# Chunks of 64 tokens in four 64x64 quadrants, two batches per step, in a written program order

## The chip, the cores and the metric

The kernel runs on one core of one Trainium2 chip. The metric is the device time of one execution in microseconds (us). Before the change, three runs took 906.59, 907.54 and 913.81 us (median 907.54). The profile comes from one further execution.

## What is computed

Two stages follow each other. The first is a recurrence over 768 tokens for 4 batches and 8 heads with a 40x40 state each; the second is a feed-forward block on the 3072 rows of 320 values that the first leaves. All inputs are fp32, except the two weight matrices, which arrive as 64-bit floats.

```python
for t in range(S):
    y[:, :, t] = einsum('bhd,bhde->bhe', r_t, state)
    Sa = einsum('bhde,bhe->bhd', state, a_t)
    state = state * w_t[:, :, None, :] - einsum('bhd,bhe->bhde', Sa, b_t)
    state = state + einsum('bhd,bhe->bhde', v_t, k_t)
x = y.transpose(0, 2, 1, 3).reshape(B * S, H * D)
h = x @ w_in                      # 320 -> 1024
solu = h * softmax(h)
ln = (solu - mean) / sqrt(var + 1e-6) * g_ln
out = ln @ w_out                  # 1024 -> 320
```

## The kernel before

The recurrence is done in chunks. Inside a chunk of 128 tokens of one batch, cumulated decays turn it into products of matrices, one triangular system per head, and a state that goes from chunk to chunk. There are 4 batches of 6 chunks, so 24 steps; consecutive steps belong to different batches.

`load` and `decay` (L240, L260) bring a chunk's inputs and make cumulated decays: `pcum` and `pcx` on TensorE, exp on ACT, and the scaled keys `kb` on GpSimd (L280). `front` (L289) transposes a and b, multiplies them to the triangular matrices `nt` with `scores`, and sends `ax`, `kb` and `nt` to DRAM. The four 32x32 diagonal blocks of each of the 8 heads go into `blk_dram`; four chunks fill its 128 rows. `invert` (L322) reads such a batch back and inverts all its blocks at once on VectorE, 30 columns with two instructions each (L336, L338), and stores the inverse `u` and its transpose. `bring` (L350) fetches everything for a chunk again. `solve` (L385) completes the 128x128 inverses from the 32x32 ones by products in 32x32 and 64x64 tiles (`py`, `pz`; L398, L424, L431). `attend` makes kT, vT, rT and the masked products `psi` and `lamv`. `recurrence` (L437) carries the state: `px`, `pu`, `pnu`, `plamu`, `pst`. `readout` (L487) makes the chunk's output `pyo`, scales it, and moves it into `xT` by DMA.

The feed-forward block is `hidden` (L510: `h` in 12 matmul records, a maximum, exp, product, statistics, normalised rows) and `output` (L544: eight transposes `plnT`, then `po` in 16 records).

`weights` (L186) fetches the two matrices in pieces on ACT's DMA queue and `narrow` (L141) turns their 64-bit words into fp32 with instructions on VectorE, GpSimd and ACT in turn. Two buffers hold the landing words.

The main loop starts several of these as generators and takes one part of each in turn. A scheduler then orders the instructions of each engine when the program is built; the only constraints written out are a barrier after the first four fronts and `tc.issue_after(inverted[0])`, which holds the weights' conversion until the first inversion is through. All of the chunk's DMAs are issued by SyncE (SP). PSUM has six single banks in rotation and one pair for `h`.

Of the kernel before, what the change touches and what calls it, by code (L numbers as in the profile page):

```python
# [16 lines left out]
P = 128  # L17
Q = 32
TILE_HEADS = ((0, 1, 6), (2, 3, 7), (4, 5))
GRP = 4  # L20
AHEAD = 6
LAG = 3
# [3 lines left out]
def shape_constants():  # L26

    s, t = np.arange(P)[:, None], np.arange(P)[None, :]
    first = (s < P // 2).astype(np.float64)
    parts = dict(
        ident=np.eye(P),
        tri=s < t,
        cum_in=first - (s <= t),
        cum_ex=(s < t) - first,  # L40
        half=np.concatenate([1 - first, first], 1),
    )
    at, where = 0, {}
    for name, x in parts.items():
        where[name] = (at, at + x.shape[1])
        at += x.shape[1]
    return np.concatenate([np.asarray(x, np.float64) for x in parts.values()], 1).astype(np.float32), where
# [3 lines left out]
def kernel(  # L51
# [18 lines left out]


# [4 lines left out]
    G = H // 2  # L76
    NCH = S // P
    N = B * NCH
    NF = DFF // P
    NK, KT = 3, 3 * D  # L80
    assert (H, D, S % P, DFF) == (8, 40, 0, 1024)

    const = ctx.enter_context(tc.tile_pool(name="const", bufs=1))
    raw = ctx.enter_context(tc.tile_pool(name="raw", bufs=2))
    two = ctx.enter_context(tc.tile_pool(name="two", bufs=2))
    small = ctx.enter_context(tc.tile_pool(name="small", bufs=4))
    dram = ctx.enter_context(tc.tile_pool(name="dram", bufs=AHEAD + 2, space=bass.MemoryType.DRAM))
    ps1 = ctx.enter_context(tc.tile_pool(name="ps1", bufs=6, space=PSUM))
    ps2 = ctx.enter_context(tc.tile_pool(name="ps2", bufs=1, space=PSUM))

    nc.scalar.preload_act_table_set(LN_EXP)

    def zeroed(engine, name, shape, n, pad=False):

        tiles = []
        for i in range(n):
            x = const.tile(shape, FP32, name=f"{name}{i}")
            if pad:
                flat = x if len(shape) == 3 else x.rearrange("p j h c -> p (j h) c")
                engine.memset(flat[:, :, D:64], 0.0)  # L100
            else:
                engine.memset(x, 0.0)
            tiles.append(x)
        return tiles

# [12 lines left out]


    lw_t = zeroed(nc.gpsimd, "lw", [P, H, 64], 2, True)  # L120
    a_t = zeroed(nc.gpsimd, "a", [P, H, 64], 2, True)
    kb_t = zeroed(nc.gpsimd, "kb", [P, 2, H, 64], 2, True)
    rv_t = zeroed(nc.vector, "rv", [P, 2, H, 64], 3, True)
    x0_t = zeroed(nc.vector, "x0", [P, H, 64], 2, True)
    ti_t = zeroed(nc.vector, "tinvT", [P, 2, G, P], 2)
    tn_t = zeroed(nc.vector, "tinv", [P, 2, G, 64], 2)
    sm_t = zeroed(nc.vector, "sm", [P, G, 2, 64], 2)
    st_t = [const.tile([P, G, D], FP32, name=f"st{i}") for i in range(B)]
    nu_t = [const.tile([P, H, 64], FP32, name=f"nu{i}") for i in range(2)]
    y_mid = const.tile([P, 2, G, Q], FP32, name="y_mid")  # L130
    y_last = const.tile([P, 2, G, 64], FP32, name="y_last")
    AXW = 2 * P + 2
# [7 lines left out]

    def narrow(dst, bits):  # L141


# [23 lines left out]
    def load_weight(dst, parts, step):  # L167

# [11 lines left out]
        if wide_:  # L180
            for lo in range(0, width, step):
                with tc.issue_after(inverted[0]):
                    narrow(dst[:, lo:lo + step], to[:, lo:lo + step])
                yield

    def weights():  # L186
# [8 lines left out]
        for c in range(NF):  # L195
            yield from load_weight(w2[:, c, :], [moe_w_out[c * P:(c + 1) * P, :]], DM)
            nc.gpsimd.tensor_scalar(out=w2[:, c], in0=w2[:, c], scalar1=g_col[:, c:c + 1],
                                    scalar2=None, op0=ALU.mult)

    def half(p):  # L200
        return slice(64 * p, 64 * p + 64)

    def pair(t, g):
        return t[:, 2 * g:2 * g + 2, :].rearrange("p a b -> p (a b)")
# [4 lines left out]
    def transposed(name, src, tag="T", bufs=3):  # L209

        t = bank("p" + name)
        for g in range(G):
            nc.tensor.transpose(out=t[:, g * P:(g + 1) * P], in_=pair(src, g), identity=ident)  # L213
        o = two.tile([P, G, P], FP32, tag=tag, name=name, bufs=bufs)
        nc.scalar.copy(out=o.rearrange("p g t -> p (g t)"), in_=t)  # L215
        return o

    def scores(name, lhs, rhs, dst):

        t = [bank("p" + name) for p in range(2)]  # L220
        for g in range(G):
            for p in range(2):
                nc.tensor.matmul(t[p][:, g * P:(g + 1) * P], lhsT=lhs[half(p), g, :],  # L223
                                 rhs=rhs[half(p), g, 0:P], start=True, stop=True)
        for p in range(2):
            nc.vector.tensor_tensor(  # L226
                out=dst[:, p], in0=t[p].rearrange("q (g c) -> q g c", g=G),
                in1=tri.unsqueeze(1).to_broadcast([P, G, P]), op=ALU.mult)

    def wide(name, bufs=2):  # L230
        return two.tile([P, 2, G, P], FP32, tag=name, name=name, bufs=bufs)

    st = [dict() for _ in range(N)]
    blocks, inverse, inverted = {}, {}, []

    def where_(i):
        ci, bi = divmod(i, B)
        return bi, ci

    def load(i, late=False, others=nc.sync):  # L240
        if i >= N:
            return
        bi, ci = where_(i)

        def src(ap):
            return ap[bi, :, ci * P:(ci + 1) * P, :].rearrange("h t d -> t h d")

        d = st[i]
        if late:
            rv = d["rv"] = rv_t[i % 3]  # L250
            nc.sync.dma_start(out=rv[:, 1, :, 0:D], in_=src(v))
            nc.sync.dma_start(out=rv[:, 0, :, 0:D], in_=src(r))
            return
        for n, ap, queue in (("w", w, nc.sync), ("b", b, nc.sync), ("k", k, others)):
            d["raw_" + n] = raw.tile([P, H, D], FP32, tag="raw_" + n, name="raw_" + n)
            queue.dma_start(out=d["raw_" + n], in_=src(ap))
        d["a"] = a_t[i % 2]
        others.dma_start(out=d["a"][:, :, 0:D], in_=src(a))

    def decay(i):  # L260

        d = st[i]
        lw, kb = lw_t[i % 2], kb_t[i % 2]
        d["kb"] = kb
        nc.scalar.activation(out=lw[:, :, 0:D], in_=d["raw_w"], func=AF.Ln)
        ax = d["ax"] = two.tile([P, G, AXW], FP32, tag="ax", name="ax")
        inv = two.tile([P, DM], FP32, tag="inv", name="inv")
        t = bank("pcum")
        nc.tensor.matmul(t[:, 0:DM], lhsT=c_("cum_in"), rhs=lw[:, :, 0:D], start=True, stop=True)
        nc.scalar.activation(out=inv, in_=t[:, 0:DM], func=AF.Exp)  # L270
        lo = where["cum_ex"][0]
        for j in range(2):
            t = bank("pcx")
            for g in range(2):
                nc.tensor.matmul(t[:, g * 130:g * 130 + 130], lhsT=pair(lw, 2 * j + g), rhs=cst[:, lo:lo + 130],
                                 start=True, stop=True)
            nc.scalar.activation(out=ax[:, 2 * j:2 * j + 2, P:], in_=t[:, 0:260].rearrange("p (g t) -> p g t", g=2),
                                 func=AF.Exp)
        for j, n in enumerate("kb"):
            nc.gpsimd.tensor_tensor(out=kb[:, j, :, 0:D], in0=d["raw_" + n], in1=heads(inv), op=ALU.mult)  # L280
    def quarter(q):
        return slice(Q * q, Q * q + Q)

    def homes(i, q):

        at = (i % GRP) * 32 + q * H
        return slice(at, at + H)

    def front(i):  # L289

        d = st[i]
        decay(i)
        yield
        ax = d["ax"]
        t = bank("paT")
        for g in range(G):
            nc.tensor.transpose(out=t[:, g * P:(g + 1) * P], in_=pair(d["a"], g), identity=ident)
        nc.vector.tensor_tensor(out=ax[:, :, 0:P], in0=t.rearrange("p (g t) -> p g t", g=G), in1=ax[:, :, P:2 * P],
                                op=ALU.mult)
        bT = transposed("bT", d["kb"][:, 1])  # L300
        d["ax_dram"] = dram.tile([P, G, AXW], FP32, tag="ax_dram", name="ax_dram")
        nc.sync.dma_start(out=d["ax_dram"], in_=ax)
        d["kb_dram"] = dram.tile([P, 2, H, 64], FP32, tag="kb_dram", name="kb_dram")
        nc.sync.dma_start(out=d["kb_dram"], in_=d["kb"])
        yield
        nt = wide("nt")
        scores("nt", bT, d["ax"], nt)
        load(i + 2)
        yield
        n = i // GRP  # L310
        if i % GRP == 0:
            blocks[n] = dram.tile([P, Q, Q], FP32, tag="blk_dram", name="blk_dram", bufs=2)
        for q in range(4):
            nc.sync.dma_start(out=blocks[n][homes(i, q)].rearrange("h s t -> s h t"),
                              in_=nt[quarter(q), :, :, quarter(q)].rearrange("s p g t -> s (p g) t"))
# [280 lines left out]
    for i in range(N):  # L596
# [4 lines left out]
        if more:  # L601
            bring(i + 1)
# [44 lines left out]
```

## Time and profile before

| | |
|---|---|
| median of the runs | 907.54 us |
| span of the profiled execution | 908.3 us |
| TensorE (PE) busy | 784.1 us, 86% |
| VectorE (DVE) busy | 487.9 us, 54% |
| ScalarE (ACT) / GpSimd (POOL) busy | 262.9 / 135.9 us |
| DMA engines, mean busy share 387 to 515 us | 0.62 |
| first `px`, last `po` records | 123.3 us, 904.5 us |
| a step between 258.8 and 706.2 us | 31.95 us |

The profiled execution took 908.3 us from first to last instruction, which is also its time. A line of a group reads: source line, engine, operation, output<-inputs, shapes, count, then busy time in us and mean ns of one, then the engine's idle time before these and what ended it. PEld is TensorE's weight load, which overlaps PE. In the chain of what ended last, each line is start, length in us, and what ran or was waited for. The clock of TensorE is a share of full speed.

### The profile page before, as it was taken

The page shows a single profiled execution, that of the slowest core. Times are in us where ns is not written, and L with a number is a line of the kernel's source. Part 1 is how long each engine was busy: PE and PEld are TensorE (multiplying, and loading weights), DVE is VectorE, ACT ScalarE, POOL GpSimd, SP SyncE. Part 2 cuts the span into 40 slices and gives each one's busy share as a digit, 9 for nine tenths or more (in the row PEclk, how much of TensorE's full clock was granted, in tenths as well). Part 3 has the DMA queues.
Part 4 walks back from the last instruction along what each step waited for, and adds up shares of the span by engine and source line. Part 5 has one row for each costly group of instructions (what it writes and reads, how often), then busy time and mean ns, then how long its engine had stood idle before and what let it go on. Part 6 is the DMA issues. An engine that isn't in the chain of part 4 may idle for free.

```text
span 908.3 us, 20640 instructions
## 1 busy us (share of the span) xinstructions
PE 784.1 (86%) x8481; PEld 605.8 (67%) x8481; DVE 487.9 (54%) x1088; ACT 262.9 (29%) x566; POOL 135.9 (15%) x176
## 2 busy tenths in 40 slices
PE   5440387885999999999999999999999999999985
PEld 4330275664877787687778678777777887776643
DVE  4139575594432795543794345965337944325322
ACT  2110342321333233243233323233232323322211
POOL 2112567211011002001001100110110010000000
PEclk9855577997899999999999999999999999999987
DMA  9996678564575745667456576545645244210000
GB/s 193 223 196 158 157 188 200 130 156 135 115 168 114 198 98 179 141 129 163 126 143 172 123 173 139 144 144 123 147 117 146 70 105 101 67 63 15 8 15 14
DMA packets 276093, 117.95 MB, mean 130 GB/s; under 512 B 251160, under 2 KB 258080, under 8 KB 276000
## 3 DMA queue, kind: packets, MB, share of 16 engines
q1 hardware_dynamic: 269728, 110.47, 50.8%
q10 hardware_dynamic: 6272, 6.17, 2.7%
q8 instruction: 67, 1.10, 0.5%
q14 instruction: 26, 0.21, 0.1%
HBM read 68.52 MB, written 44.14 MB: 124 GB/s over the span
## 4 chain that ended last, share of the span: by engine, by line
PE 61%; DVE 15%; DMA 9%; issue 5%; POOL 4%; SPq 3%; ACT 2%; POOLq 0%; ACTq 0%; DVEq 0%
PE po L558 12%; PE h L517 10%; DVE u L338 4%; PE pyo L498 4%; DVE prod L336 4%; PE px L451 4%; PE plnT L553 3%; DMA kbx<-kb_dram 3%; PE py L424 2%; PE ppsi L223 2%; PE pyo L494 2%; PE pnt L223 2%; PE pu L458 2%; PE pst L474 2%; DMA bits<-in_moe_w_out_dram 2%
## 5 line engine op out<-in xcount | busy, mean ns | idle before, releaser
L517 PE MATMUL h<-w_in,xT 120*128 120x512 f32 (+1 forms) x288 | 148.3, 641 | 9.5 <-issue 5.7
L558 PE MATMUL po<-w,lnT 128*128 128x320 f32 x384 | 111.4, 444 | 0.0
L226 DVE TENSOR_TENSOR psi<-ppsi,cst 128x512 f32<-128x512 f32 x48 | 30.9, 684 | 122.1 <-PE ppsi L223 122.1
L558 PEld LDWEIGHTS po<-w,lnT 128*128 128x128 f32 x384 | 72.3, 193 | 30.1 <-issue 2.4
L517 PEld LDWEIGHTS h<-w_in,xT 120*128 120x128 f32 (+1 forms) x288 | 51.6, 197 | 54.5 <-issue 49.9
L539 POOL TENSOR_TENSOR rs<-c,mhalf 128x1 f32<-128x1 f32 x24 | 13.2, 549 | 428.7 <-DVE c L538 428.7
L521 DVE TENSOR_REDUCE nmax<-h 128x1 f32<-128x1024 f32 x24 | 29.4, 1223 | 72.0 <-PE h L517 72.0
L213 PE MATMUL pkT<-cst,kbx 128*128 128x128 f32 x96 | 16.3, 295 | 57.0 <-DMA kbx<-kb_dram 55.4
L338 DVE TENSOR_TENSOR u<-u,prod 128x30 f32<-128x30 f32 (+9 forms) x180 | 62.4, 347 | 4.6
L336 DVE TENSOR_TENSOR prod<-blk,u 128x30 f32<-128x30 f32 (+9 forms) x180 | 61.7, 343 | 5.1
L213 PEld LDWEIGHTS pkT<-cst,kbx 128*128 128x128 f32 x96 | 11.9, 150 | 69.4 <-issue 58.9
L215 ACT COPY kT<-pkT 128x512 f32<-128x512 f32 x24 | 14.0, 585 | 133.1 <-PE pkT L213 131.9
L554 ACT COPY lnT<-plnT 128x512 f32<-128x512 f32 x48 | 26.0, 588 | 90.3 <-PE plnT L553 90.3
L451 PE MATMUL px<-rv,psi 128*128 128x40 f32 x384 | 47.7, 286 | 0.0
L451 PEld LDWEIGHTS px<-rv,psi 128*128 128x128 f32 x384 | 46.8, 199 | 0.0
L280 POOL TENSOR_TENSOR kb<-raw_k,inv 128x320 f32<-128x320 f32 x24 | 21.0, 874 | 162.5 <-issue 113.0
L498 PE MATMUL pyo<-lamv,kbx 128*64 128x128 f32 x384 | 42.2, 282 | 0.0
L498 PE MATMUL pyo<-lamu,kbx 128*64 128x128 f32 x384 | 41.0, 273 | 0.0
L433 DVE TENSOR_SCALAR tinvT<-pz 64x256 f32<-64x256 f32 x48 | 19.7, 413 | 36.6 <-PE pz L431 36.0
L223 PE MATMUL pnt<-ax,bT 64*128 64x128 f32 x384 | 31.2, 297 | 7.5 <-ACT bT L215 3.9
L226 DVE TENSOR_TENSOR lamv<-plamv,cst 128x512 f32<-128x512 f32 x48 | 30.9, 684 | 11.1 <-PE plamv L223 11.1
L424 PEld LDWEIGHTS py<-tinv,ntx 64*64 64x64 f32 x384 | 25.6, 142 | 16.7 <-issue 9.1
(110 smaller groups left out, 1549.7 us busy)
## 6 DMA issues: line engine op xcount, KB each, us to landing
ax_dram<-ax SPq DMA_DIRECT2D x24, 516.0 KB
axx<-ax_dram SPq DMA_DIRECT2D x24, 516.0 KB
kb_dram<-kb SPq DMA_DIRECT2D x24, 512.0 KB
kbx<-kb_dram SPq DMA_DIRECT2D x24, 512.0 KB
nt_dram<-nt SPq DMA_DIRECT2D x24, 192.0 KB
ntx<-nt_dram SPq DMA_DIRECT2D x24, 192.0 KB
raw_w<-in_w_dram SPq DMA_DIRECT2D x24, 160.0 KB
raw_b<-in_b_dram SPq DMA_DIRECT2D x24, 160.0 KB
```

The source lines that it names most:

```text
L213: nc.tensor.transpose(out=t[:, g * P:(g + 1) * P], in_=pair(src, g), identity=ident)
L223: nc.tensor.matmul(t[p][:, g * P:(g + 1) * P], lhsT=lhs[half(p), g, :], rhs=rhs[half(p), g, 0:P], start=True, stop=True)
L226: nc.vector.tensor_tensor(out=dst[:, p], in0=t[p].rearrange("q (g c) -> q g c", g=G), in1=tri.unsqueeze(1).to_broadcast([P, G, P]), op=ALU ...
L336: nc.vector.tensor_tensor(out=t, in0=nb[:, j:j + 1, j + 1:Q].to_broadcast([P, j, m]), in1=u[:, 0:j, j:j + 1].to_broadcast([P, j, m]), op=A ...
L338: last = nc.vector.tensor_tensor(out=u[:, 0:j, j + 1:Q], in0=u[:, 0:j, j + 1:Q], in1=t, op=ALU.subtract)
L424: nc.tensor.matmul(t[hi, g * 64:g * 64 + 64], lhsT=nt[lo, G * p + g, 32:96], rhs=tinv[lo, p, g, :], start=True, stop=True)
L451: nc.tensor.matmul(t[:, h * D:h * D + D], lhsT=d["psi"][:, h % 2, h // 2, :], rhs=vb[:, h, 0:D], start=not ci and h == 0, stop=True, skip_ ...
L498: nc.tensor.matmul(t[half(h % 2), h // 2 * P:h // 2 * P + P], lhsT=kb[:, j, h, :], rhs=lam[:, h % 2, h // 2, :], start=not ci and h < 2 an ...
L517: nc.tensor.matmul(h[:, hh], lhsT=d["xT"][0:n, kt, :], rhs=w_in[0:n, kt, hh], start=kt == 0, stop=kt == NK - 1)
L521: nc.vector.tensor_reduce(out=nmax, in_=h, axis=AX.X, op=ALU.max, negate=True)
L553: nc.tensor.transpose(out=t[:, j * P:(j + 1) * P], in_=ln[:, f * P:(f + 1) * P], identity=ident)
L558: nc.tensor.matmul(o[:, 0:DM], lhsT=lnT[:, f, :], rhs=w2[:, f, :], start=f == 0, stop=f == NF - 1)
```

## The change

A chunk is now 64 tokens, and one step takes the same chunk of two batches, one on partitions 0 to 63 and one on 64 to 127. Again there are 24 steps: two pairs of batches in turn, 12 chunks each. Every product between 64-token matrices is 64x64 (contraction of 40 or 64) and is addressed to one of TensorE's four quadrants; `in_turn` orders 16 such products so that the four quadrants alternate. There are 13 groups of 16 in a full step (`carried`, `norm`, `driven`, `solved` twice, `couple`, `answered`, `scores` twice, `read` three times, `close`).

With 64 tokens the inverse has two 32x32 diagonal blocks and one off-diagonal block, so one `couple` and one `close` complete it. `nt`, the transposed a and the decays stay in SBUF; only `kb` makes the round trip through DRAM. The state is no longer scaled to mid-chunk: decays count from the chunk's start, and the state's transposes are made by `states`. The state update is read off the same PSUM tile as the output (`read`, columns 64 to 103).

Loads are split by batch and, for v and r, by head parity: 16 DMAs for the six inputs instead of six. `invert` keeps its arithmetic and its four-chunk batches; its pieces are called by `some` at fixed places. Normalisation after the statistics is left out of VectorE: the mean over 1024 is taken out of `w2` once, and 1/sqrt is applied by ACT as it copies `po`.

The pools run under `manual_schedule`: all engines execute in the order in which the Python code issues. `fence` puts a marker on GpSimd between groups that write one PSUM tile from different quadrants.

```diff
-AHEAD = 6
-LAG = 3
+C = 64
+AHEAD = 7
+    ctx.enter_context(tc.manual_schedule())
...
+    units = [(p, g, q, h) for g in range(2) for p in range(2) for q in range(2) for h in range(2)]
+    def in_turn(tile_of, some=units):
+        lots = {}
+        for u in some:
+            lots.setdefault(tile_of(*u), []).append(u)
+        lots = list(lots.values())
+        return [lot[n] for n in range(max(map(len, lots))) for lot in lots if n < len(lot)]
...
+    def fence(tiles):
+        for t in tiles:
+            nc.gpsimd.keepalive_nop([nc.gpsimd.lower_ap(t[:, 0:512])])
...
+    def fetch(i):
+        d["kb"] = two.tile([P, 2 * H, C], FP32, tag="kbx", name="kbx")
+        nc.sync.dma_start(out=d["kb"], in_=d["kb_dram"])
...
+    def driven(i):
+        for u in in_turn(lambda p, g, q, h: (p, p ^ h)):
+            p, g, q, h = u
+            j = 2 * g + q
+            mm(d["px"][h][half(p ^ h), j * D:j * D + D], d["psi"][half(p), h, j],
+               d["lv"][half(p), 4 * h + 2 * g + q, C:], start=(h, p ^ h) not in d["opened"])
+            d["opened"].add((h, p ^ h))
...
+    first = -(AHEAD + 2)
+    for i in range(first, N + 2):
+        j = i + AHEAD
+        n, at = divmod(j, GRP)
+        early = i < 0
+        if i == first:
+            load_keys(0)
+            load_keys(1)
+        carried(i)
+        norm(j)
+        driven(i)
+        load_keys(j + 3)
+        load_values(i + 2)
+        spread(j)
+        if ok(j) and at == GRP - 1:
+            inv[0] = invert(n)
+            some(1)
+        folded(i - 2)
+        attend(i + 1)
+        some(3)
+        fetch(i + 2)
+        output(i - 2)
+        solved(i)
+        couple(i + 1)
+        some(3)
+        hidden(i - 1)
+        answered(i)
+        weighed(i - 1)
+        scores(i + 1)
+        spreadof(i - 1)
+        some(3)
+        front(j + 1)
+        decay(j + 2)
+        states(i + 1)
+        some(3)
+        if early:
+            drawn(5)
+        read(i, True)
+        close(i + 1)
+        read(i, False)
+        leave(i)
+        if (i + 2) % GRP == 0:
+            some(40)
+        if i == -1:
+            drawn(100)
+        bring(i + 2)
```

In it, `spread` sends a chunk's diagonal blocks to `blk_dram`; the first piece of `invert` (`some(1)`) loads a full batch and makes `u<-blk` on VectorE; `folded` and `output` are the two halves of the old `output`; `weighed` and `spreadof` are the product and the statistics of the old `hidden`; `leave` scales the output, issues the four `xT` DMAs and updates the state (sums on VectorE, product on GpSimd); `drawn` takes pieces of `weights`; `bring` fetches a chunk's inverse blocks. Step i also does the front for chunk i + 8, and the feed-forward block for chunks i - 1 and i - 2.

## The prediction

> **What bounds the kernel now.** I read the page first, then the windows by stage, the chain of one steady step, the groups of instructions by line, and SyncE's timeline. The page names the busy engine:
>
> ```profile
> span 908.3 us, 20640 instructions
> ...
> PE 784.1 (86%) x8481; PEld 605.8 (67%) x8481; DVE 487.9 (54%) x1088; ACT 262.9 (29%) x566; POOL 135.9 (15%) x176
> ```
>
> By stage (columns: window, length, busy PE, PEld, DVE, ACT, POOL with counts, TensorE clock, DMA share, GB/s):
>
> ```profile
> 90.00:125.00 35.00, 17.32 (x180) 15.92 (x180) 21.84 (x58) 10.89 (x29) 19.34 (x22) 0.51 0.73 165
> 125.00:160.00 35.00, 26.78 (x323) 21.02 (x323) 23.52 (x54) 13.36 (x33) 26.15 (x25) 0.85 0.76 189
> 450.00:482.00 32.00, 31.51 (x366) 24.94 (x366) 26.59 (x68) 10.72 (x24) 5.42 (x6) 1.00 0.57 152
> ```
>
> Up to about 165 us the weights, which arrive as 64-bit words, are made into fp32; TensorE waits. From 258.8 to 706.2 (the starts of px L451 in the chain) 14 steps take 31.95 us each, and TensorE is busy all of it. So a steady step is worth what its TensorE instructions cost. The chain inside one step (start, length, what):
>
> ```profile
> 468.09 0.63 PE pz L398 x48
> 468.72 4.50 PE po L558 x16
> 473.23 1.07 PE py L424 x16
> 474.30 1.05 PE h L517 x2
> 475.35 1.07 PE pz L431 x16
> 476.43 3.63 PE h L517 x8
> 480.06 0.44 PE pkT L213 x4
> ```
>
> An fp32 product leaves two records, a transpose one. In one 64x64 quadrant a record costs 1.07/16 = 67 ns. The 32x32 products that go round three tiles cost 0.63/48 = 13 ns, so records of different tiles do overlap. The large products, 4.5 (po) and 5.5 (h), stay. Vector work and SyncE's issues:
>
> ```profile
> L226 DVE TENSOR_TENSOR psi<-ppsi,cst 128x512 f32<-128x512 f32 x48 | 30.9, 684 | 122.1 <-PE ppsi L223 122.1
> ...
> L338 DVE TENSOR_TENSOR u<-u,prod 128x30 f32<-128x30 f32 (+9 forms) x180 | 62.4, 347 | 4.6
> L336 DVE TENSOR_TENSOR prod<-blk,u 128x30 f32<-128x30 f32 (+9 forms) x180 | 61.7, 343 | 5.1
> ```
>
> ```profile
> 404.18 0.83 SPq L506 DMA_DIRECT2D xT<-x  x1
> ...
> 410.33 0.37 SPq L369 DMA_DIRECT2D kbx<-kb_dram  x1
> 410.79 1.39 SPq L356 DMA_DIRECT2D tinv<-ut_dram  x3
> ```
>
> An issue costs SyncE 0.37 to 0.83 us. In the chain, blocks land 2.0 us after the issue (tinv, 736.6) and 512 KB 4.0 us (kbx, 218.3).
>
> **What the skill says.** The Trainium skill, "TensorEngine Tiling (Array Packing)", Key Properties: tiles load weights and multiply in parallel, and a change of tiling mode drains the array. The 13 ns agree with the first; no row isolates the second, and I allow 1.5 us a step. "Perfetto Trace Analysis", Tensor Engine Instruction: ACT and DVE are strict FIFO. "DMA: Bandwidth & Descriptors", Anatomy of one DMA: a semaphore wait is held by the issuing sequencer, before dispatch. Before leaves its queues to a scheduler that puts inversion work into DVE's gaps (4.6 us of idle before 180 instructions), so the trace shows little of such blocking.
>
> **TensorE's part.** Per step the change has 208 small products, 416 records, over four quadrants. At 67/4 = 17 ns for 64 columns (slightly less for 32 and 40; 25 ns for 104, from pyo's 61 ns on two column tiles) they cost 7.2 us. Seven sets of four transposes at 0.5 (0.44 to 0.60 in the chain) are 3.5, plnT 1.0, po 4.5, h 5.5, pcum 0.6, drains 1.5: 23.8 us against 31.9. Bounds for a record: 13 ns (nothing but issue) and 34 ns (two at a time). I take 17. That gain of 8 us has to pass three waits that the written order creates.
>
> **A step without inversion.** T is the end of the previous step's last read product. carried and norm end at 1.1. driven waits for a marker on POOL that stands behind the state update, itself behind DVE's leave: four products of 104x128 (0.29, scaled from 413 ns for 64x256) and two sums (0.32, L480) to 1.9, POOL 0.9 (L280: 874 ns) and the marker to 3.0. driven 3.5, folded 4.6; kbx lands by 4.8; attend 6.3, output 10.8, solved 11.9, couple 12.4, hidden 17.9. DVE's reduce ends at 19.1, exp at 20.5 (L524, 1.13 + 0.21). ACT then has ex 0.59, bT 0.59, lw 0.47: 22.3; pcum 22.9, inv 23.4, POOL's two kb products 25.2, the second marker, and the last 32 read records: 26.2 us. That is 5.7 better than before.
>
> **Inversion steps.** Batches of four chunks are inverted as before: 60 small DVE instructions. The order puts u<-blk right behind norm's masks on DVE, so everything after it waits for the block transfer, and the reduce of hidden first of all. On SyncE that transfer stands behind 38 issues which cannot begin before T: fetch(i+2) waits for the last read, because kbx has two buffers. From T: fetch, two stores and kb_dram 1.5; xT (x is ready at 1.3) 3.1; bring 8 x 0.5; keys 8 x 0.45; values 8 x 0.45; spread 6 x 0.5; 0.7 for waits on the eight DMA semaphores: 19.5. Landing 2.0, the block's 512 KB 4.0: 25.5. Then u 0.7, memset 0.1 and twelve inversion instructions 3.5: the reduce ends at 31.1 where 19.1 was free, so the step is 12.1 longer: 38.3. Bounds: nothing, if the block lands before 13.6; 16 if transfers crowd, or if the clock falls in the wait (it reads 0.51 where TensorE is half idle, 90 to 125 us).
>
> In this step and the next, twelve more instructions (5.2 us) stand on DVE before leave: masks end at 23.5, statistics 25.5, six 28.1, aT 28.8, six 31.4, where TensorE had finished at 26.2. leave, POOL's update and driven shift by about 5; less a kbx wait of 0.2, 4.9 in each of two following steps. Bounds 0 and 5.2. In the last step of a group the inverse is stored and fetched through the same queue: 2.5 (0 to 4).
>
> A group of four: 38.3 + 31.1 + 31.1 + 28.7 = 129.2, 32.3 a step. The whole 6-us gain is returned.
>
> **The sum.** Weights: a w_in piece is a 4-us transfer, 0.9 of issue, and 6.1 of DVE-POOL-ACT in turn (two pieces of 0.41 + 1.11 + 0.42 + 0.42 + 0.53, overlapping), 11 us; six are 65. Eight of w2 at 7.8 are 62. The next transfer is issued behind the last ACT instruction of the piece before, so there is no prefetch. With 8 us ahead: 135. Add 13 (four exposed front stages of 3.3), 6 (first piece behind the loads), 8 (first inversion), 3 (the mean taken from w2): 165. Then inversion's end 4.5, POOL copy 1.9, store 2.7, bring 6, couple to close 5: step 0 starts at 185; before, px starts at 123.
> Steps 0 to 3, with less to do (no output yet, SyncE not yet blocked): 107. Steps 4 to 15: 388. Steps 16 to 19, no front any more: 119. 20 to 23: 101. Tail (xT 4, h 5.4, softmax 4, plnT and copy 1.7, po 4.5, store 3): 23. Sum 923; I say 922. It is made against the profiled span, 908.3, which is 0.1% from the median 907.5, so nothing is added.
>
> **Removed at no gain of their own.** The ax_dram and nt_dram round trips, the ln product (821 ns a step on DVE; its factor moves into ACT's copy of po, its mean into w2), the masks at half width: all hidden behind TensorE before; they shorten DVE but not the waits above. Without that cover DVE, 26.6 of 32 us in an inversion step, would have been next.
>
> **Rivals.** Faster: the block transfer does not hold the reduce. SyncE would have to get through 38 issues in 7 us less, or overlap their waits. For it: 8 DMAs in flight and a DMA share of only 0.57 before. Against it: 0.37 us is the cheapest issue shown, 14 us for 38 of them alone. Three full delays of 12.1 and one of 6.5 gone give 879; the DVE tails gone as well (48 in all), 831. It is on the other side: it decides from a landing at about T + 20 on.
> Startup shorter: if weights land in 3 us and fronts hide, 14 x 1.2 + 8 = 25 less, 897.
> Quadrants do not do what is said: two at a time, 34 ns, adds 7 us a step but hides behind the block wait in a quarter of them: near 1050. Against: 13 ns above.
>
> **Chances.** Forecast 0.50 (own range 900 to 958), faster rival 0.32, startup 0.13, quadrants 0.05. Measured noise of this kernel is about 1%: same is 898.5 to 916.6. Faster: 0.32 and part of startup, 0.37; same 0.12; slower 0.51. The range reaches 862 to 975, leaving out the 831 end and the quadrant case.
>
> **What would show it.** Right: the transfer blk<-blk_dram ends DVE waits before u<-blk, and the reduce behind it is about 12 us late three times and 6 once; TensorE's busy share falls well under 86%; steps alternate 26 and 38 us; driven px waits on POOL; steps start near 185. Wrong: TensorE busy over 90% in steady slices, quadrant stages well over 0.6 us per 32 records, or first px before 150.

## The result and the profile after

The change made the kernel slower: 964.73 us (median of four runs, 964.46 to 965.61) against 907.07 for the kernel before beside it (905.93 to 913.81). The ratio is 1.061, 95% interval 1.057 to 1.065. The forecast was 922.0, in a range of 862 to 975: the direction is right, the size is not (1.6% forecast, 6.1% measured).

The head of the page of the changed kernel:

```profile
span 963.8 us, 27077 instructions
...
PE 645.0 (67%) x11449; PEld 479.1 (50%) x11449; DVE 388.8 (40%) x1046; ACT 248.1 (26%) x616; POOL 146.9 (15%) x191
```

TensorE's work fell by 139 us (784.1 to 645.0), as the change meant it to. The span grew by 55.5 all the same, so no engine sets the time any more: waits do. Where they are is seen when the steps are laid side by side. As a mark of step i I take the start of ACT's copy `x<-px`, right behind the driven products. The first such copy of the kernel before, in ACT's timeline:

```profile
126.08 0.46 ACT L454 COPY x<-px 128x320 f32<-128x320 f32 x1
```

The start of step 0 moved from 126.1 us to 177.9, 52 us, which is nearly the whole loss; steps 4 to 15 take 399.2 us, 33.3 a step against 31.95 before. So the 8 us that TensorE saved in each step are gone, and the start pays on top.

Three steps in the windows between marks (window, length, busy PE, PEld, DVE, ACT, POOL, TensorE's clock, DMA share, GB/s): step 11 without inversion work, step 12 that takes in an inverse block (a block step from here on), step 21 near the end.

```profile
545.65:572.42 26.77, 22.68 (x483) 16.66 (x483) 8.79 (x23) 9.52 (x25) 4.52 (x8) 1.00 0.51 127
572.42:621.09 48.67, 27.91 (x483) 20.81 (x483) 18.65 (x50) 9.72 (x24) 3.69 (x6) 0.76 0.36 94
859.92:887.30 27.38, 23.15 (x437) 17.76 (x438) 7.51 (x20) 7.62 (x19) 1.68 (x3) 0.81 0.23 54
```

The first is what the change should give everywhere: 26.8 us with 22.7 us of TensorE. The second has the same 483 matmul records and is 22 us longer; at its mean clock of 0.76 these keep TensorE busy for 5.2 us more. The third has fewer records and no inversion, and is not shorter: its clock reads 0.81.

What holds the second stands in the chain of waits of that step (start, length, what):

```profile
571.47 0.38 SPq L395
...
581.12 0.70 SPq L247
...
591.57 0.61 SPq L257
...
597.62 3.22 DMA blk<-blk_dram
```

in TensorE's timeline, the product that the reduce of hidden needs:

```profile
586.19 5.42 PE L599 MATMUL h<-w_in,xT 120*128 120x512 f32 x12
```

and in VectorE's timeline (the bracket is the engine's idle time before the instruction, and what ended it):

```profile
600.93 0.69 DVE L350 TENSOR_SCALAR u<-blk 128x1024 f32<-128x1024 f32 x1 [28.93 <-DMA blk<-blk_dram]
...
605.03 1.22 DVE L602 TENSOR_REDUCE nmax<-h 128x1 f32<-128x1024 f32 x1
```

The previous step's last read product ended at T = 569.74 (the start of the next step's `px<-st,aT`). SyncE, still busy with the spreading transfers of step 11, issued kbx at 571.47, then 37 more transfers, and came to the block at 597.62. The block itself landed 3.2 us later. VectorE stood at `u<-blk` for 28.9 us with the reduce of hidden behind it, though h was complete at 591.6, 13.4 us before the reduce. Over the whole kernel, in the waits view (us, times, longest):

```profile
DVE u L350 <- DMA blk<-blk_dram: 146.5, 6, 31.9
...
PE px L212 <- POOLq L217: 36.7, 20, 3.6
PE pyo L212 <- POOLq L217: 31.2, 20, 3.3
```

### The profile page after: what moved, and what is told of

The parts are those of the page before. It is cut to its first block, busy times and chain, and to the rows that moved or that the text cites. A ratio compares the mean times of both kernels' runs of the same rounds, so it can differ in the third digit from the quotient of the medians.

```text
span 963.8 us, 27077 instructions
## 1 busy us (share of the span) xinstructions
PE 645.0 (67%) x11449; PEld 479.1 (50%) x11449; DVE 388.8 (40%) x1046; ACT 248.1 (26%) x616; POOL 146.9 (15%) x191
## 3 DMA queue, kind: packets, MB, share of 16 engines
q1 hardware_dynamic: 242784, 74.64, 33.3%
## 4 chain that ended last, share of the span: by engine, by line
PE 26%; issue 22%; DVE 20%; SPq 11%; DMA 9%; POOL 7%; ACT 4%; ACTq 0%; POOLq 0%; DVEq 0%
PE h L599 7%; PE po L649 6%; DVE prod L358 4%; SPq L257 3%; DVE u L360 3%; POOL n_scale L144 2%; PE pyo L212 2%; PE plnT L639 2%; DVE nmax L602 2%; DMA blk<-blk_dram 2%; SPq L247 2%; DMA bits<-in_moe_w_in_dram 2%; DVE e L611 2%; ACT e L605 2%; DVE bs L619 2%
## 5 line engine op out<-in xcount | busy, mean ns | idle before, releaser
L267 PE MATMUL pcum<-lw,cst 128*128 128x320 f32 x48 | 26.6, 647 | 97.4 <-ACT lw L265 97.4
L605 ACT ACTIVATE e<-h,nmax 128x1024 f32<-128x1024 f32 x24 | 26.8, 1116 | 195.6 <-DVE nmax L602 195.6
L212 PE MATMUL pyo<-lv,kbx 64*64 64x104 f32 x768 | 43.6, 295 | 43.5 <-POOLq L217 31.2
L350 DVE TENSOR_SCALAR u<-blk 128x1024 f32<-128x1024 f32 x6 | 4.2, 694 | 146.5 <-DMA blk<-blk_dram 146.5
L212 PEld LDWEIGHTS pyo<-lv,kbx 64*64 64x64 f32 x768 | 27.6, 159 | 47.3 <-POOLq L217 33.5
L212 PE MATMUL px<-lv,psi 64*64 64x40 f32 x768 | 22.2, 275 | 36.9 <-POOLq L217 36.7
L212 PE MATMUL pyo<-lu,kbx 64*64 64x104 f32 x768 | 42.4, 289 | 0.7 <-DVE lu L304 0.5
L639 PE MATMUL plnT<-cst,e 128*128 128x128 f32 x192 | 40.2, 376 | 3.9 <-DVE e L611 3.9
L212 PE MATMUL pnt<-aT,bT 40*64 40x64 f32 x768 | 20.9, 259 | 28.2 <-DVE aT L299 27.7
L212 PEld LDWEIGHTS px<-lv,psi 64*64 64x64 f32 x768 | 19.7, 185 | 39.4 <-issue 34.1
L280 PE MATMUL pkT<-cst,kbx 128*104 128x128 f32 x96 | 22.7, 382 | 23.0 <-DMA kbx<-kb_dram 22.9
```

The lines of the kernel that those rows point to most:

```text
L212: nc.tensor.matmul(o, lhsT=lhsT, rhs=rhs, start=start, stop=stop, skip_group_check=True)
L267: nc.tensor.matmul(t[:, 0:DM], lhsT=c_("cum"), rhs=lw, start=True, stop=True)
L280: nc.tensor.transpose(out=t[0:W2, j * P:(j + 1) * P], in_=pair(src_, 2 * j), identity=ident)
L605: nc.scalar.activation(out=e, in_=h, func=AF.Exp, bias=nmax, accum_out=d["esum"])
L639: nc.tensor.transpose(out=t[:, j * P:(j + 1) * P], in_=d["e"][:, f * P:(f + 1) * P], identity=ident)
```

## The experiments

**Theories.** A: the loss is made by the written order: a block transfer behind SyncE's issues that holds VectorE's queue, inversion columns and markers ahead of what TensorE needs, and a start in which weights are converted one instruction after another. Rival B: the quadrant products or the changes of tile cost TensorE more than priced. Rival C: the transfers themselves are slow, not their place in the order. Sums come from the profiled executions, by the mark above.

| kernel | median, us | ratio to before (95%) | step 0 starts | steps 0-3 | steps 4-15 | steps 16-22 |
|---|---|---|---|---|---|---|
| the change | 964.7 | 1.061 (1.057-1.065) | 177.9 | 130.1 | 399.2 | 206.7 |
| e1 block first | 930.9 | 1.019 (1.014-1.025) | 190.5 | 118.4 | 371.3 | 199.7 |
| e3 columns early | 957.3 | 1.049 (1.044-1.053) | 181.9 | 125.8 | 394.3 | 203.9 |
| e4 block late | 922.0 | 1.011 (1.006-1.016) | 176.0 | 122.6 | 375.7 | 198.1 |
| e5 prefetch | 962.2 | 1.054 (1.050-1.059) | 174.5 | 128.0 | 401.6 | 206.5 |
| e6 one quadrant | 1016.4 | one run | 184.1 | 132.9 | 434.9 | 214.2 |
| e8 markers first | 917.4 | 1.005 (1.003-1.008) | 178.5 | 126.3 | 382.9 | 179.0 |
| e9 weights in pairs | 930.7 | 1.019 (1.014-1.025) | 151.3 | 122.4 | 396.8 | 205.1 |
| e10 late and early | 865.1 | 0.949 (0.944-0.955) | 175.3 | 115.1 | 331.5 | 191.3 |
| e12 pairs, no prefetch | 940.4 | 1.032 (1.027-1.037) | 160.8 | 122.5 | 400.2 | 205.0 |
| e13 root only | 945.6 | 1.037 (1.032-1.042) | 178.8 | 127.5 | 398.9 | 193.6 |
| e14 order mended | 827.1 | 0.906 (0.901-0.911) | 172.6 | 113.3 | 327.1 | 161.4 |
| e15 all mended | 795.8 | 0.872 (0.868-0.875) | 148.9 | 100.1 | 334.3 | 161.9 |

The kernel before had medians of 907 to 913 us in the four series, so differences in us under about 6 are not read.

**e1, the block's transfers ahead of the loads.**

```diff
-        load_keys(j + 3)
-        load_values(i + 2)
         spread(j)
         if ok(j) and at == GRP - 1:
             inv[0] = invert(n)
             some(1)
+        load_keys(j + 3)
+        load_values(i + 2)
```

> The six spreading transfers and the block transfer go ahead of the sixteen loads of keys and values in SyncE's order; nothing else changes. Theory A (issue order on SyncE holds DVE's queue): sixteen issues of about 0.65 us, 10.4 us, leave the way of the block, so the wait of u<-blk on its transfer falls from 31.9 us at most to about 21, steps 4, 8 and 12 fall from about 44.6 to about 34, step 0 by 10 and step 16 by 8: 50 us, 915 in all. Rival B (the quadrant products and the changes of mode cost TensorE more than priced): no change, 965. Rival C (the transfers' landing, not their issue, is slow): the block now shares the DMA engines with the loads or lands when it did; less than 15 us gained, over 950.

Measured 930.9, 34 us less; 50 were expected. Steps 4, 8 and 12 lost 9.6, 10.1 and 10.6 us and step 0 10.3, as theory A had it; step 16 only 3.9, and step 0 started 12.6 us later, since in the early iterations the loads now stand behind the spreading transfers, which wait for masks on VectorE (19.3 us at once before 156.1, in SyncE's waits). The wait of `u<-blk`, in the waits view of this kernel:

```profile
DVE u L350 <- DMA blk<-blk_dram: 99.6, 6, 20.5
```

146.5 became 99.6. The same transfers moved the same bytes; only their order differs. That speaks for A over C, as does the block's own transfer, 3.2 us of a wait of 28.9; B has nothing to say to it.

**e3, the inversion columns ahead of the reduce.**

```diff
         attend(i + 1)
-        some(3)
+        some(6)
...
         couple(i + 1)
-        some(3)
+        some(6)
...
         spreadof(i - 1)
-        some(3)
...
         states(i + 1)
-        some(3)
```

> The four slots of three inversion columns each become two of six, both ahead of the reduce of hidden; none stands between the statistics and leave. Theory A: the two steps behind each inversion step lose about 4.9 us each, and the inversion step gains 3.5 because six columns more stand ahead of its reduce: 6.3 less per group, five groups, 31 us less, about 933. If a column after the statistics costs nothing (TensorE is not waiting for leave): 965 plus five times 3.5, 982. Rival B: no change, 965.

A gain of 7 (8 between the profiled executions), not 31: steps 5, 9 and 13 fell by 4.7 to 6.3 us as expected, but the block steps grew by 0.9 to 1.4 and the step after next by up to 3.6. PE's timeline of this kernel names two of the reasons:

```profile
346.15 1.09 PE L280 MATMUL paT<-cst,a 128*104 128x128 f32 x4 [18.92 <-DVE lu L304]
387.51 0.62 PE L280 MATMUL pkT<-cst,kbx 128*104 128x128 f32 x4 [2.97 <-DMA kbx<-kb_dram]
```

In the block step all twelve columns now stand between the block and the reduce, and paT waits 18.9 us for what follows the reduce (14.3 with the change). And once leave was no longer late, step 6 waited 3.0 us for kbx; with the change pkT of this step has no such wait. The columns' place costs, but it can't be mended while the block holds the queue in front of them.

**e4, VectorE's part of the inversion one step after its transfer.**

```diff
         nc.sync.dma_start(out=nb, in_=blocks[n])
+        yield
...
-        some(3)
+        some(0 if ok(j) and at == GRP - 1 else 4)
```

> The block transfer is issued where it was, behind all loads, but the vector instructions that need it come one step later: no inversion work in the step of the transfer, four columns per slot in place of three in the next two. Theory A (DVE's queue stood behind the block): steps 4, 8 and 12 fall from 44.6 to about 27, step 0 by 15, step 16 by 9, 77 us in all; the columns pushed into the next two steps give back about 4 us per group: near 908. Rival B: no change, 965. Rival C (the wait is one of TensorE or ACT on another transfer of the same crowded queue): the step stays over 38, over 940.

With VectorE's part go the twelve columns of the block step, which are shared out over the next two steps. The transfer is issued as late as before, and the steps that issue it are now short: steps 4, 8 and 12 take 29.7, 26.6 and 28.2 us (48.3, 46.9 and 48.7 with the change), step 0 22.7 instead of 43.3. Of the 146.5 us that `u<-blk` waited, 18.2 are left:

```profile
DVE u L351 <- DMA blk<-blk_dram: 18.2, 4, 8.5
```

This is the plainest evidence for A: nothing but the place in VectorE's queue needed the block so early. The columns that moved can account for 8.7 us, by the prices in the forecast (3.5 and 5.2), of the 18.6 to 20.5 us by which steps 4, 8 and 12 fell. But the two steps behind rose by 11.5 to 14.2 us together, 922 and not 908. VectorE's timeline of step 9 shows how:

```profile
471.90 1.23 DVE L603 TENSOR_REDUCE nmax<-h 128x1 f32<-128x1024 f32 x1 [11.40 <-PE h L600]
...
478.71 0.35 DVE L359 TENSOR_TENSOR prod<-blk,u 128x184 f32<-128x184 f32 x1
...
487.02 0.88 DVE L571 TENSOR_TENSOR x<-pyo,ex 104x128 f32<-104x128 f32 x4
```

VectorE idles for 11.4 us ahead of the reduce, and between the statistics and leave (`x<-pyo`) eight columns take most of 8.3 us. The time for the columns was there, a few us earlier.

**e10, the same with the columns in that idle time.**

```diff
         attend(i + 1)
-        some(0 if ok(j) and at == GRP - 1 else 4)
+        some(0 if ok(j) and at == GRP - 1 else 8)
...
         couple(i + 1)
-        some(0 if ok(j) and at == GRP - 1 else 4)
+        some(0 if ok(j) and at == GRP - 1 else 8)
...
         spreadof(i - 1)
-        some(0 if ok(j) and at == GRP - 1 else 4)
...
         states(i + 1)
-        some(0 if ok(j) and at == GRP - 1 else 4)
```

> As e4_block_late, but the inversion columns of the two following steps all stand ahead of the reduce of hidden, eight in each of two slots, where DVE was idle for 11.4 us; none stands between the statistics and leave. Theory A (it is the place on DVE's queue that costs): the two steps behind each inversion step fall from 37.5 and 32.5 to about 27 to 28, 75 us for five groups: 845 to 865. If a column costs its time wherever it stands: no change from 922.

865.1, at the edge of A's forecast and 5.1% faster than the kernel before. In VectorE's timeline sixteen columns, 11 us from 433.3 on, are through before h comes, and the engine idles again:

```profile
443.76 0.41 DVE L361 TENSOR_TENSOR u<-u,prod 128x240 f32<-128x240 f32 x1
449.74 1.22 DVE L603 TENSOR_REDUCE nmax<-h 128x1 f32<-128x1024 f32 x1 [5.57 <-PE h L600]
```

The steps behind the block step are now 24.8 to 32.6 us (32.3 to 37.6 in e4). So e3 and e4 are not to be added (7 and 43): each leaves the other's delay standing. Together 100. This is what the Trainium skill says of ACT and DVE as strict FIFO ("Perfetto Trace Analysis", Tensor Engine Instruction), priced: one wait and 60 small instructions per batch cost 100 us more, over six batches, in one place of the order than in another.

**e6, one quadrant after the other.**

```diff
-        return [lot[n] for n in range(max(map(len, lots))) for lot in lots if n < len(lot)]
+        return [u for lot in lots for u in lot]
```

> The units of every set of small products are issued quadrant by quadrant, all of one quadrant before the next, in place of in turn; the same instructions otherwise. Theory A (products of different quadrants overlap; 17 ns a record comes from four at once): a record of 64 columns goes back towards the 67 ns of the kernel before, 416 records cost about 20 us more a step, less what the block wait hides: 1300 to 1400 in all. Rival B (quadrants do not overlap more than issue would give anyway): the records stay at about 17 ns, 965.

1016.4 us: quadrants do overlap. First the pu products of the change in PE's timeline, then of this kernel in its chain:

```profile
527.85 0.69 PE L212 MATMUL pu<-tinvT,x 64*64 64x64 f32 x32
528.37 0.63 PE L212 MATMUL pu<-x,tinvT 64*64 64x40 f32 x32
```

```profile
519.63 2.34 PE pu L212 x61
```

From start to start 32 records take 0.52 us in turn, 16 ns each; quadrant by quadrant a record takes 2.34/61 = 38 ns on average. The starts of the single records in the traces tell what this average is made of. In both kernels the eight records of one quadrant start 58 ns apart (107 from the first to the second). In turn, four such rows run side by side, 7 ns apart. Quadrant by quadrant, a row starts 0.29 us behind the row ahead of it, which has three records to go, so neighbouring quadrants still overlap. So 38 ns is not the cost of a record in one quadrant; 58 is. The `py` records of the kernel before also start 58 ns apart; my 67 was 1.07/16, which counts the length of the last record in. Theory A had the right mechanism, but neither of its consequences, 67 ns and 1300 us, came, because this order does not keep to one quadrant at a time. TensorE's busy time per full step rose from 22.7 to 29.3 us at full clock; 24 times 6.6 us would be 158, the kernel is 52 slower, so two thirds hide behind other waits. Rival B is out: in turn, 16 ns is what I had priced (17).

**e8, POOL's markers ahead of POOL's work; e13, the second half of it alone.** The state update moves from leave to behind the marker of carried; the root `rs` from spreadof to behind the marker of the read products.

```diff
         carried(i)
+        update(i - 1)
...
         read(i, True)
+        root(i - 1)
```

> On POOL the state update moves behind the marker of the carried products, and the root of the variance behind the marker of the read products; nothing else. Theory A (TensorE waits for POOL's queue, 36.7 us before driven products and 31.2 before read products): about 1 us less a step from the update, 2 to 3 us less in the eight last steps from the root; 935 to 950. Rival (the markers wait for TensorE itself, POOL's order is free): no change, 965.

> Only the second half of e8_markers_first: the root of the variance moves behind the marker of the read products; the state update stays ahead of the marker of the carried products. If the 47 us of e8 came from the root alone (the read marker behind DVE's statistics): 915 to 925. If from the state update alone (the driven products behind leave): 955 to 965. By the waits of the changed kernel (31.2 us for the read marker, 36.7 for the driven marker) about half each: near 940.

e8 takes off 47 us, more than forecast; e13 alone 19, less than half. The waits of e13 say why half an edit gave less than half:

```profile
PE px L212 <- POOLq L217: 50.8, 19, 7.4
```

The read marker's wait is gone, but TensorE now comes to the driven marker earlier and waits there: 36.7 us had been, 50.8 are. In e8 it is 8.1, and the read marker's wait is gone too: of 67.9 us for the two markers 8.1 are left, where I had counted on 15 to 30 us of gain. The clock adds to that. PE's timeline of the change in a late step, and the windows around it, each 3.41 us long, the grid on which the clock of this trace changes:

```profile
855.35 0.63 PE L212 MATMUL pyo<-lv,kbx 64*64 64x104 f32 x8 [2.73 <-POOLq L217]
...
858.75 1.09 PE L212 MATMUL px<-lv,psi 64*64 64x40 f32 x32 [0.92 <-POOLq L217]
```

```profile
850.49:853.90 3.41, 1.92 (x92) 1.60 (x84) 3.24 (x7) 1.05 (x5) 0.00 (x0) 1.00 0.02 5
853.90:857.31 3.41, 1.97 (x56) 1.97 (x56) 1.28 (x7) 0.00 (x0) 0.55 (x1) 0.50 0.00 0
857.31:860.73 3.42, 2.50 (x57) 2.30 (x54) 1.11 (x6) 0.49 (x2) 1.13 (x2) 0.50 0.71 217
860.73:864.14 3.41, 3.41 (x18) 3.32 (x17) 0.00 (x0) 2.34 (x4) 0.00 (x0) 0.50 0.20 48
864.14:867.56 3.42, 3.42 (x14) 2.46 (x14) 0.00 (x0) 0.58 (x1) 0.00 (x0) 1.00 0.31 49
```

The clock falls in the midst of the wait, behind a window in which TensorE was busy for 1.92 us of 3.41. It comes back behind the first window that TensorE fills, so it reads 0.50 for 10.2 us; the rest of the wait and the second one, 0.92 us for the driven marker, lie in between. In this trace all 33 falls follow a window with TensorE busy for at most 60%, all 33 rises one with at least 85%. Late steps take 26.6 to 27.4 us with TensorE busy 23.2 to 23.6 at a mean clock of 0.81 in the change, and 22.4 to 23.8 with 20.3 to 21.7 at 0.93 to 0.97 in e8: some 2 us of each gain are clock. The Trainium skill ("TensorE: Matmul & The Clock Gate", What's actually happening) says that about 3.4 us of idle halve the clock and that one busy stretch as long gives it back. The second agrees with the window from 860.73 to 864.14. For the first, less was enough here: TensorE was idle for 1.5 us of the window ahead of the fall.

**e5, e9 and e12, the weights.** e5 issues a piece's transfer before the narrowing of the piece ahead of it; e12 narrows two halves of a piece with alternating instructions, those of one half in a somewhat changed order; e9 does both.

```diff
+        ahead = load_weight(*jobs[0][:3])
+        for k, job in enumerate(jobs):
+            now, ahead = ahead, load_weight(*jobs[k + 1][:3]) if k + 1 < len(jobs) else None
...
-                narrow(dst[:, lo:lo + step], to[:, lo:lo + step])
-                yield
+            two_ = [narrow(dst[:, lo:lo + width // 2], to[:, lo:lo + width // 2]) for lo in (0, width // 2)]
+            for _ in range(5):
+                for x in two_:
+                    next(x)
```

> The transfer of each weight piece is issued before the narrowing of the piece ahead of it, so that it lands meanwhile; the rest of the order stays. If the weights' serial chain of transfer, then narrowing, sets the start: fourteen pieces lose most of a 3 to 4 us transfer, step 0 starts at about 135 and not at 177, about 925 in all. If the narrowing on three engines, or SyncE's backlog, sets the start: under 10 us, over 955.

> The alternating halves of e9_weights_in_pairs without the early transfers. If the two delays stand in one chain and hide each other (early transfers alone gave 2.5 us, both 34): the halves alone leave a 3 to 4 us transfer ahead of each of 14 pieces, step 0 starts at 160 to 177, 945 to 965. If the halves carry it all: start near 151, 931.

> On top of the early weight transfers, each weight piece is made into fp32 as two halves whose instructions alternate on the three engines, in place of one chain after the other. If the chain of DVE, POOL and ACT in turn sets the start: w_in pieces fall from about 9 us to 6, w2 pieces from 5.8 to about 4.5, step 0 starts near 145 and not 174, about 935 in all. If POOL's own work (about 70 us before step 0) or the first inversion and its stores set it: start over 165, over 950.

The early transfers alone moved the start by 3.4 us, and the time by no more than the runs can tell. The chain of e5 at the start shows what then stands in the way, one engine after the other, for one half of a piece:

```profile
63.24 0.42 ACT n_scale L145
63.66 0.32 ACT n_man L148
64.00 0.42 DVE n_man L150
64.42 0.35 DVE n_scale L151
64.84 0.72 POOL w_in L153
```

The halves alone give 24 us (start 160.8), both edits 34 (start 151.3). So the transfers matter only when the chain of instructions no longer covers them. The start still lies 25 us behind the kernel before, whose scheduler converts weights beside the first steps until about 165 us; that part was not tried here.

**e14 and e15, the versions that the experiments point to.** e14 is e10 and e8 together, e15 adds e9.

> e10_late_and_early and e8_markers_first together: block late, columns ahead of the reduce, markers ahead of update and root. Theory A: e10 still waits 32.6 us for the read marker and 15.6 for the driven one; most of these 48 us go: 820 to 835. If the two edits buy the same time: 860.

> As e14_order_mended, and the weights in alternating halves with early transfers, as e9. Theory A (start and steps are separate terms of the sum): 34 us less than e14, 785 to 800, 13% under the kernel before. If the weights then collide with what moved: 815 to 830.

827.1 and 795.8 us: both as forecast, 9.4% and 12.8% faster than the kernel before, with the quadrants and a written order kept. The head of e15's page:

```profile
span 791.0 us, 27199 instructions
...
PE 595.9 (75%) x11449; PEld 434.1 (55%) x11449; DVE 390.9 (49%) x1086; ACT 249.0 (31%) x632; POOL 152.0 (19%) x207
```

The same 11449 matmuls keep TensorE busy for 595.9 us and not 645.0: this is clock. Worked out from the clock over each record, the half clock adds 107 us to TensorE's busy time in the change and 48 in e15, more than the difference.

## Why the prediction was right or wrong

The terms of its sum, by the mark above:

| term | forecast | measured |
|---|---|---|
| step 0 starts | 185 | 178 |
| steps 0 to 3 | 107 | 130 |
| steps 4 to 15 | 388 | 399 |
| steps 16 to 19 | 119 | 125 |
| 20 to 23 and tail | 124 | 131 |
| sum | 923 | 964 |

**Right: TensorE's part.** 23.8 us a step forecast; 22.7 measured at full clock. The quadrant record is 16 ns (17 taken). A step without inversion was to take 26.2; steps 6, 10 and 14, the shortest of their groups, take 25.5 to 25.9.

**Right: the block holds VectorE and the reduce behind it.** e4 takes most of the wait away (18.2 us of 146.5 are left) and moves the columns that hang on it, and the long steps become short.

**Wrong, the step that failed: "Steps 0 to 3, with less to do (no output yet, SyncE not yet blocked): 107".** 107 is what four steps of 26.2 and the 2.5 of a group's last step come to. So for these four steps the forecast put two delays at nothing that it had worked out for the later groups: the wait for the block, and the columns ahead of leave. Step 0 has the same wait, and longer than any other, in VectorE's and SyncE's timelines:

```profile
210.16 0.69 DVE L350 TENSOR_SCALAR u<-blk 128x1024 f32<-128x1024 f32 x1 [31.95 <-DMA blk<-blk_dram]
```

```profile
165.84 0.32 SPq L382 DMA_DIRECT2D ul<-ut_dram  x1
...
206.84 0.34 SPq L347 DMA_DIRECT2D blk<-blk_dram  x1
```

SyncE was not held by a last read product there, but by its own backlog: bring waited for the first inverse's stores until 165.8, and everything queued behind it was issued almost without a pause until 207. Step 0 takes 43.3 us; with VectorE's part moved out of it, in e4, it takes 22.7, though the steps behind it grow. The four steps take 130.1 us with the change; counted like a later group, 129.2, the term would have come within 1 us, in part by luck, since step 0 waits for another reason. The 23 us that it lacks are over half of what the forecast missed. e10, where the wait is gone and the columns have a better place, takes 15 of them off (115.1).

**Mis-sized: the way to the block.** The issue of the block was forecast at T + 21.5 and measured at T + 27.9 (26.7 and 27.7 in steps 8 and 4). The sixteen loads take 11.1 us (581.12 to 592.18) and not 7.2, since one of these issues costs 0.62 to 0.67 us (medians over the trace) and not 0.45; kbx, out and kb_dram are through at T + 4.0 and not 1.5; the spread takes 4.0 and not 3.0; the 0.7 for semaphores was too much. The transfer itself takes 3.2 and not 4.0. I took 0.45 from the kernel before though its own rows spread from 0.37 to 0.83. With that, the reduce ends at T + 36.5 instead of 31.1. From T to T the block steps 4, 8 and 12 take 44.6, 43.7 and 45.6 us, not 38.3; in step 12 the late reduce makes 5.4 of this. Over each group of four steps this makes 33.3 us on the mean, not 32.3.

**Right: the columns ahead of leave.** From T to T, as the forecast counts, the two steps behind a block step take 29.2 to 31.1 us; 31.1 was forecast for each. By the mark, which stands behind the late leave, the first of the two delays falls into the block step: 38.3 + 4.9 = 43.2 was forecast there, 46.9 to 48.7 measured, and the third step of a group shows none. But "less a kbx wait of 0.2" was too small: 3.0 us showed in e3 as soon as leave came earlier.

**Mis-sized: the late steps.** I gave them 25.2 us with no front in the way. They take 26.6 to 27.4, because the root's place on POOL holds the read products for 2.7 us and the clock halves; with the root alone moved, in e13, steps 20 to 22 take 23.1 to 25.5. The clock was in the forecast only as a bound of the block step, though the windows of the kernel before showed 0.51 where TensorE is half idle; it belonged into the late steps too.

**Nearly right, for a wrong reason: the start.** 185 forecast, 178 measured, but I counted a transfer of 4 us without prefetch in each piece on top of the narrowing. e5 issues the transfers early and gains 3.4 us at the start; e12 shortens the narrowing alone and gains 17.1. The chain of narrowing was the bound.

**Rivals.** The faster rival needed a landing at about T + 20; it was T + 31. "Startup shorter" had a part in it, 7 us. "Two at a time, 34 ns" did not come; e6 brings about that average (38 ns), and the kernel then takes 1016, not the 1050 that I gave.

**Left open.** Why e3's fourth step of a group lengthened by 1.5 us in two groups, what follows the late reduce in step 12 (1.9 us), and e15's start, 23 us behind the kernel before. e6 is a single run. A third kbx buffer, which would free SyncE from the last read product, was not tried.

## What to carry to other kernels

When an order is written by hand, list for each in-order queue (SyncE's too, and markers on an idle engine) what stands behind every instruction that may wait; an instruction should be placed where its operand is due, not where its transfer is issued. Edits that mend one queue show little alone when the next queue waits for the same step, so mend them together before judging one, and check the very first step by itself.

## What was not expected of the hardware

A wait can cost TensorE more than itself: the clock read 0.50 for 10.2 us around a 2.7-us wait, in each of the late steps. The records of one 64x64 quadrant start 58 ns apart, alone or with three other quadrants beside them: 32 records in turn take 0.52 us where 32 times 58 ns would be 1.86, an estimated gain of 3.6. Written quadrant by quadrant they still average 38 ns, since neighbours overlap. An issue on SyncE for the loads (64 partitions, rows of 160 bytes) takes 0.62 to 0.67 us whether a partition has 4 or 8 rows, against 0.34 for the 512-KB block.
